# Value sums divided in the tail by spread inverse denominators, stacked rows sent one transfer at a time, and gate rows in three buffers

## The chip, the cores and the metric

The kernel runs on one core of a Trainium2 chip. The time is device time in microseconds (us), the median of several executions of the whole program. One execution is also recorded by the hardware profiler; it gives the rows quoted below. Engines are called by the profile's names: PE (matrix products; PEld is its weight load), DVE (vector), ACT (scalar), POOL (GpSimd), SP (the queue that issues nearly all DMAs here). A queue runs its instructions in order: an instruction that waits holds up all that stand behind it on the same queue.

## The reference, cut to what matters

```
g = sigmoid((x * gate_w).sum(-1, keepdims=True))           # x: 2048 x 512
qkv = x @ wqkv;  H = 32 heads, Dh = 16, window W = 256
scores = q k^T * Dh**-0.5, kept where 0 <= i - j < 256
o = softmax(scores) @ v                                      # per head
a = o.reshape(2048, 512) @ wo
b = (silu(x @ w_gate) * (x @ w_up)) @ w_down                 # F = 1792
return g * a + (1 - g) * b
```

A softmax is a sum of exponentials times values, divided by the sum of the exponentials. The kernel obtains both sums from the same matrix product: every head's values carry one more column of ones, so that of the 32 rows of a head in the result 16 are value sums and row 16 (`DH`) is the denominator.

## The kernel before

All products are made from pairs of fp32r halves (a high part and a remainder, `split`, three matmuls for one). 2048 tokens are 16 blocks of 128 (`NB`) or 4 chunks of 512 (`NCH`); the 32 heads are 8 groups of 4 (`G`); the 1792 hidden columns are 14 tiles (`NF`) with a gate and an up half each, 28 units.

1. Prologue (to about 127 us): x and the weights are loaded and split, V is made and stored to DRAM (`vd`), and Q and K are made for all groups by a product scheme with fewer multiplications. Each Q/K piece goes to a DRAM buffer (`xd`).

2. Lead-in, 64 ticks (about 127 to 188 us). A tick is one pass of the emitting loop: three steps of the FFN stream (`stream`, `unit`, `lanes`, matmuls at L483, copies of finished sums to SBUF tiles `ev` at L510 on ACT, stores to DRAM `raws` at L511 on SP) and, from tick 10 on, pieces of `stage1` of group 0 (row maxima of the scores, L539 on PE, L541 on DVE). Beside it the rows of Q and K are brought back from `xd` into tiles of stacked operands by `stack`: 12 DMAs of 128 KB for each half of a group, issued on SP at L320 and L322. The ring of `ev` tiles has `EV` = 5 buffers (`kept`).

3. Main part, 8 groups of 64 ticks (about 188 to 660 us). In group g each tick holds a quarter of `stage1` of group g + 1, a quarter of `stage2` of group g (scores again, L578, exponentials on ACT, L580, masks on POOL, L582 and L585) and 9/4 FFN steps on average. Every 16 ticks `av` makes the value sums of one chunk (L602), and `evacuate` moves them: PSUM tile `second` by ACT to `ob` (L615), PSUM tile `first` by DVE to `oe` (L616), their sum by POOL into `ob` (L619). `ob` has one buffer. `finish` divides, one chunk later, beside the evacuation of the next chunk: ahead of it DVE transposes 32 x 32 blocks of `ob` (L626), inverts the denominators (L629) and multiplies (L630), and two ticks behind it DVE transposes back into `oe` (L633) and POOL stores `oe` to DRAM `od` (L634). So the next copy into `ob` (L615 on ACT) waits for L626 on DVE. FFN steps around `av` are (2, 1, none, 2) at the four ticks and 4 right after `av`.

4. In the last group there is no `stage1`. In its place 8 of the 14 down weights are loaded into slots that have become free (`wd_early`, through `kept()` tiles, split by DVE 4 ticks later), three hidden tiles are begun (`tile_load`, `tile_early`, L694 on ACT), and the gates are made: `gate_block` loads 128 rows of x into the tile `xn` (L667, 256 KB) and 3 ticks later multiplies them with `gw` and sums on DVE (L668), 16 times. `xn` has one buffer, and the loads begin 5 ticks ahead of the last group.

5. Tail (about 660 us to the end). `step` multiplies the 14 hidden tiles of each chunk with the down weights, 12 matmuls of 128 x 512 a step (L79 to L81). For each step SP loads 512 KB of `raws` (`got`, L830), ACT and DVE make the hidden tile (L835, L836) and split it (L67, L70). During the first chunk the other six down weights and the four parts of `wo` are loaded through `raw2` (3 buffers) and split. `load_oc` brings back the attention output from `od` (L795); `attn_split` and `attn_out` project it, chunk 0 during chunk 1 and each later chunk at its own end. SP and DVE run ahead of PE by at most the buffers of `got` (4) and `hp` (3).

The order on every queue is the order of emission; `at(k, f)` and `later(n, f)` put work at a tick.

## Time and profile before

| | us |
|---|---|
| median of 3 runs | 868.2 (866.72 to 868.23) |
| the profiled execution, its own time | 870.03 |
| its span, first to last instruction | 868.0 |
| PE / DVE / ACT / POOL busy in the span | 834.5 / 579.1 / 465.5 / 376.0 |
| mean granted clock of PE | 0.986 |

A view by stretches gives, for a stretch of the span, the busy time of each engine with the number of its instructions, then the granted PE clock (1.00 is full), the mean share of the DMA engines and the rate. A timeline row is: start, duration, engine, line, operation, out<-in, count, and in brackets how long the engine had been idle before it and what ended the wait. A row of waits is: who waited <- for what: us in total, times, longest. A row of a group is: line, engine, operation, tiles, shapes, count | busy us in total, mean ns of one | idle time before. A row of the chain of waits has only start, duration, and what.

### The profile page before, as it was taken

To read this page: it belongs to the slowest core of one execution; us is meant where nothing else is said; L and a number is where in the kernel's file an instruction comes from. 1 tells how busy PE (TensorE), PEld (TensorE's weight loads), DVE (VectorE), ACT (ScalarE), POOL (GpSimd) and SP (SyncE) were. 2 spreads that over 40 slices of the span, in tenths; PEclk is the share of its full clock that TensorE was granted. 3 is DMA by queue.
4 is the path that set the end of the run, shared out by engine and by line. 5 is a ranking of instruction groups with operands and counts; after the bars stand their busy time and mean duration, and the time that the engine had idled before them with its cause. 6 is when DMAs were issued, how large, how long until landed. Compare 5 with 4: busy or idle time off the path is not lost.

```text
span 868.0 us, 20987 instructions
## 1 busy us (share of the span) xinstructions
PE 834.5 (96%) x7897; PEld 687.4 (79%) x7897; DVE 579.1 (67%) x1504; ACT 465.5 (54%) x947; POOL 376.0 (43%) x667
## 2 busy tenths in 40 slices
PE   9999999699999999999999999997878899999998
PEld 7888887598787788878887878785757688888886
DVE  5665524477888888888888888883665855254543
ACT  7455541136666676666675766664545453334341
POOL 5124465025656575565665655654643121102010
PEclk9999999899999999999999999999888999999999
DMA  8346678642544456345543554345556886375561
GB/s 297 128 169 235 249 259 279 203 136 84 175 149 160 134 167 201 109 158 177 171 156 118 187 177 135 130 129 178 167 176 222 291 269 206 100 242 169 179 185 48
DMA packets 78820, 154.20 MB, mean 178 GB/s; under 512 B 12352, under 2 KB 16832, under 8 KB 78720
## 3 DMA queue, kind: packets, MB, share of 16 engines
q1 hardware_dynamic: 74752, 138.97, 49.6%
q0 software_dynamic: 3968, 13.90, 4.3%
q8 instruction: 62, 1.02, 0.6%
q14 instruction: 38, 0.31, 0.1%
HBM read 88.34 MB, written 64.49 MB: 176 GB/s over the span
## 4 chain that ended last, share of the span: by engine, by line
PE 80%; DMA 5%; DVE 5%; POOL 3%; SPq 2%; issue 2%; ACT 1%; DVEq 0%; POOLq 0%; ACTq 0%
PE pb L483 15%; PE pa L483 15%; PE ps L602 8%; PE ps L539 6%; PE ps L81 5%; PE ps L79 5%; PE ps L80 5%; PE ps L578 4%; DMA xn<-xn 3%; PE ps L368 3%; PE ps L208 3%; PE pa L368 2%; PE pb L368 2%; PE pb L79 2%; PE pb L80 2%
## 5 line engine op out<-in xcount | busy, mean ns | idle before, releaser
L541 DVE CUSTOM_DVE_ANT_0 ps<-ps,mask 128x384 f32<-128x384 f32 (+2 forms) x512 | 269.8, 545 | 73.4 <-PE ps L539 28.9
L580 ACT ACTIVATE pt<-ps 128x384 f32<-128x384 f32 (+2 forms) x512 | 234.4, 478 | 99.9 <-PE ps L578 55.1
L578 PE MATMUL ps<-q,k 64*128 64x384 f32 (+2 forms) x512 | 166.7, 346 | 13.9 <-ACT pt L580 13.7
L539 PE MATMUL ps<-k,q 63*128 63x384 f32 (+2 forms) x512 | 163.1, 336 | 2.9 <-DVE mx L541 0.6
L582 POOL TENSOR_SCALAR_AFFINE_SELECT pt<-pt 128x256 f32<-128x256 f32 x256 | 106.9, 417 | 118.6 <-ACT pt L580 116.2
L539 PEld LDWEIGHTS ps<-k,q 63*128 63x128 f32 x512 | 92.4, 184 | 31.7 <-DVE mx L541 22.8
L578 PEld LDWEIGHTS ps<-q,k 64*128 64x128 f32 x512 | 94.2, 186 | 25.8 <-ACT pt L580 19.9
L483 PE MATMUL pb<-xhi,wh 64*128 64x512 f32 x432 | 106.8, 409 | 5.3 <-ACT ev L510 5.3
L483 PE MATMUL pa<-xhi,wh 64*128 64x512 f32 x432 | 104.8, 407 | 1.6 <-ACT ev L510 1.6
L483 PE MATMUL pb<-xlo,wh 64*128 64x512 f32 x432 | 105.2, 400 | 0.0
L483 PE MATMUL pb<-xhi,wl 64*128 64x512 f32 x432 | 103.8, 397 | 0.0
L483 PE MATMUL pa<-xlo,wh 64*128 64x512 f32 x432 | 102.6, 398 | 0.0
L483 PE MATMUL pa<-xhi,wl 64*128 64x512 f32 x432 | 100.7, 395 | 0.0
L585 POOL TENSOR_SCALAR_AFFINE_SELECT pt<-pt 128x256 f32<-128x256 f32 x224 | 96.0, 429 | 0.0
L836 DVE TENSOR_TENSOR sg<-got,sg 128x512 f32<-128x512 f32 x53 | 47.6, 898 | 70.4 <-ACT sg L835 57.7
L602 PE MATMUL ps<-pt,vg 64*32 64x320 f32 (+4 forms) x2816 | 77.7, 350 | 0.0
L602 PEld LDWEIGHTS ps<-pt,vg 64*32 64x32 f32 x2816 | 50.8, 106 | 28.4 <-issue 10.4
L619 POOL TENSOR_TENSOR ob<-oe,ob 128x512 f32<-128x512 f32 x32 | 41.8, 1306 | 71.1 <-DVE oe L616 56.1
L541 DVE DVE_READ_ACCUMULATOR2_ANT mx<- 128x1 f32 x512 | 72.2, 141 | 0.0
L483 PEld LDWEIGHTS pb<-xhi,wh 64*128 64x128 f32 x432 | 56.6, 188 | 11.6 <-ACT ev L510 6.2
L483 PEld LDWEIGHTS pa<-xhi,wh 64*128 64x128 f32 x432 | 54.3, 189 | 7.3 <-issue 3.0
L483 PEld LDWEIGHTS pb<-xhi,wl 64*128 64x128 f32 x432 | 57.5, 188 | 3.1
(230 smaller groups left out, 1683.9 us busy)
## 6 DMA issues: line engine op xcount, KB each, us to landing
raws<-ev SPq DMA_DIRECT2D x112, 256.0 KB
got<-raws SPq DMA_DIRECT2D x106, 256.0 KB
q<-xd SPq DMA_DIRECT2D x96, 128.0 KB
k<-xd SPq DMA_DIRECT2D x96, 128.0 KB
xd<-cx SPq DMA_DIRECT2D x16, 512.0 KB
xd<-cy SPq DMA_DIRECT2D x16, 512.0 KB
od<-oe POOLq DMA_DIRECT2D x32, 256.0 KB, 3.1
raw<-wgu SPq DMA_DIRECT2D x28, 256.0 KB
```

The costliest lines, as they stand in the source:

```text
L79: nc.tensor.matmul(ps, lh, rh, start=start and i == 0, stop=False, skip_group_check=skip)
L80: nc.tensor.matmul(ps, lh, rl, start=False, stop=False, skip_group_check=skip)
L368: nc.tensor.matmul(ps, l[:, w], r[:, k], start=n in (1, 2, 5) and k == m == 0, stop=k == 1 and m == 2, skip_group_check=True)
L483: mm = nc.tensor.matmul(ps[me], w[r], x[r], start=not second and i == 0, stop=bool(second) and i == n - 1)
L539: nc.tensor.matmul(ps[:, :n], QT[g % 2][pr][r, q0:q0 + P], KT[g % 2][pr][r, k0:k0 + n], start=True, stop=True)
L541: mx = nc.vector.tensor_tensor_reduce(out=ps[:, :n], in0=ps[:, :n], in1=mask[:, 3 * P - n:], scale=1.0, scalar=NEG, op0=ALU.add, op1=ALU.m ...
L578: nc.tensor.matmul(ps[:, :n], KT[g % 2][pr][r, k0:k0 + P], QT[g % 2][pr][r, k0:k0 + n], start=True, stop=True)
L580: BEHIND.append(nc.scalar.activation(pt[:, j, :n], ps[:, :n], AF.Exp, scale=SCALE))
L582: nc.gpsimd.affine_select(out=pt[:, :, :P], in_=pt[:, :, :P], pattern=[[0, 2], [1, P]], compare_op=ALU.is_ge, fill=0.0, base=0, channel_mu ...
L585: nc.gpsimd.affine_select(out=pt[:, :, 2 * P:], in_=pt[:, :, 2 * P:], pattern=[[0, 2], [-1, P]], compare_op=ALU.is_ge, fill=0.0, base=-1, ...
L602: nc.tensor.matmul(AV[g, c][h][32 * j:32 * j + 32, q0 - c * CH:q1 - c * CH], VG[4 * g + kb // 4][o, kb % 4, 17 * j:17 * j + 32], PT[g, kb, ...
L836: nc.vector.tensor_tensor(out=sg, in0=gu[1], in1=sg, op=ALU.mult)
```

## The change

- `finish` is gone. `evacuate` adds the two parts into `oe`, and POOL stores the undivided sums with their denominators to `od` at once.
- In the tail the denominators of a chunk (32 heads x 512) are loaded as a 128 x 128 tile (`load_den`, 64 KB), inverted by DVE (`put_den`), stored to DRAM (`rd`, 64 KB), and loaded back with each row repeated for the 16 rows of its head (`load_rd`, four DMAs of 256 KB a chunk, into the tiles of x that are no longer used). `attn_split` multiplies on DVE before it splits. `load_den` and `put_den` stand at steps 4 to 8 of the first chunk, `load_rd` beside each `load_oc`.
- `stack` yields after each DMA, and `spread` issues one DMA every tick or every second tick.
- `EV` is 7 in place of 5.
- The gates' rows go into three quarters of the slot `k01`, which is free in the last group; the loads begin one tick into that group, one every 3 ticks, and the products come 6 ticks after their load. Down weights 6 and 7, which had that slot, are loaded at ticks 54 and 58 of the group.
- The FFN steps around `av` are (2, 1, 2, 2) and 2 right after it.

```diff
@@ -26,7 +26,7 @@
 NSLOT = 4
 NEG = -1.0e30
 SCALE = DH ** -0.5
-EV = 5
+EV = 7
 SYNC = mybir.DependencyInfo(mybir.DependencyClass.Sync, mybir.DependencyReason.DATA)
 
 
@@ -47,6 +47,7 @@
     vd = dram.tile([G, P, NB, VW], F32, name="vd")
     od = dram.tile([G, P, S], F32, name="od")
     raws = dram.tile([NF, 2, NCH, P, CH], F32, name="raws")
+    rd = dram.tile([NCH, H, CH], F32, name="rd")
     xd = [[dram.tile([2, P, 2 * CH], F32, name=f"xd{g}{hf}") for hf in range(2)] for g in range(G)]
 
     gate = const.tile([P, NB], F32, name="gate")
@@ -318,8 +319,10 @@
             q, k = (halves_of(t[g % 2][pr])[hf] for t in (QT, KT))
             for b, w in enumerate((0, 1, 0)):
                 nc.sync.dma_start(q[b::4].bitcast(F32), xd[g][hf][w, 32 * pr:32 * pr + 32])
+                yield
             for b, w in enumerate((0, 0, 1)):
                 nc.sync.dma_start(k[b::4].bitcast(F32), xd[g][hf][w, 64 + 32 * pr:96 + 32 * pr])
+                yield
 
     SOON, AT_PRODUCT = {}, [0]
 
@@ -424,9 +427,9 @@
                     if i == j:
                         constant_rows(0, 0, (name,), nc.gpsimd)
                 if i == 7:
-                    stack(0, 0, (0,))
+                    run(stack(0, 0, (0,)))
                 if i == 11:
-                    stack(0, 0, (1,))
+                    run(stack(0, 0, (1,)))
                 if i == 10:
                     prepare()
             step_end()
@@ -458,6 +461,9 @@
 
         def at(k, *fs):
             AT.setdefault(k, []).extend(fs)
+
+        def spread(k, n, gen):
+            at(k, lambda: None if next(gen, run) is run else spread(k + n, n, gen))
 
         def tick_end():
             for f in AT.pop(NOW[0], ()):
@@ -604,35 +610,16 @@
                                          PT[g, kb, j // 2][o, j % 2, q0 - kb * P:q1 - kb * P],
                                          start=n == 0, stop=n == len(orders[0]) - 1, skip_group_check=True)
 
-        AB = {}
-
         def evacuate(g, c):
 
             first, second = AV[g, c]
             lo = 0 if c else 64
             e = osb.tile([P, CH], F32, name="oe", bufs=2)
-            b = osb.tile([P, CH], F32, name="ob")
-            nc.scalar.copy(b[:, lo:], second[:, lo:])
+            o = osb.tile([P, CH], F32, name="ob")
+            nc.scalar.copy(o[:, lo:], second[:, lo:])
             nc.vector.tensor_copy(e, first)
-            if lo:
-                nc.gpsimd.memset(b[:, :lo], 0.0)
-            nc.gpsimd.tensor_tensor(out=b, in0=e, in1=b, op=ALU.add)
-            AB[g, c] = e, b
-
-        def finish(g, c):
-
-            e, b = AB.pop((g, c))
-            ot = osb.tile([P, CH], F32, name="ot")
-            nc.vector.transpose(ot, b)
-            v = ot.rearrange("p (s e) -> p s e", e=32)
-            rc = osb.tile([P, CH // 32], F32, name="rc")
-            nc.vector.reciprocal(rc, v[:, :, DH])
-            nc.vector.tensor_tensor(out=v[:, :, :DH], in0=v[:, :, :DH],
-                                    in1=rc[:, :, None].to_broadcast([P, CH // 32, DH]), op=ALU.mult)
-            yield
-            nc.vector.transpose(e, ot)
+            nc.gpsimd.tensor_tensor(out=e[:, lo:], in0=e[:, lo:], in1=o[:, lo:], op=ALU.add)
             nc.gpsimd.dma_start(od[g, :, c * CH:(c + 1) * CH], e)
-            yield
 
 
 
@@ -647,11 +634,14 @@
             run(steps, 3)
             if n == 1:
                 constant_rows(1, 0, ("q00", "k00", "q01", "k01"), nc.gpsimd)
-                stack(0, 1)
+                spread(n - TICKS + 1, 1, stack(0, 1))
             if n in (8, 10, 12, 14):
                 hf, pr = divmod(n // 2 - 4, 2)
                 constant_rows(hf, 1, (f"q1{pr}", f"k1{pr}"), nc.gpsimd)
-                stack(1, hf, (pr,))
+            if n == 15:
+                spread(n - TICKS + 1, 2, stack(1, 0))
+            if n == 40:
+                spread(n - TICKS + 1, 2, stack(1, 1))
             if n == 40:
                 put_max(0, 0)
             if n >= 48 and n % 4 == 0:
@@ -660,12 +650,16 @@
         run(first)
         put_max(0, 1)
 
-        gwb = osb.tile([P, D], F32, name="gwb")
+        GT = []
+
+        def gate_place():
+            GT.extend(h for piece in halves_of(slot("k01", F32)) for h in halves_of(piece))
+            nc.sync.dma_start(GT[0], gw[None, :].to_broadcast([P, D]))
 
         def gate_block(b):
-            t = osb.tile([P, D], F32, name="xn")
+            gwb, t = GT[0], GT[1 + b % 3]
             nc.sync.dma_start(t, xn[b * P:(b + 1) * P])
-            later(3, lambda: nc.vector.scalar_tensor_tensor(t, t, 1.0, gwb, op0=ALU.mult, op1=ALU.mult,
+            later(6, lambda: nc.vector.scalar_tensor_tensor(t, t, 1.0, gwb, op0=ALU.mult, op1=ALU.mult,
                                                             accum_out=gate[:, b:b + 1]))
 
         def gate_end():
@@ -714,23 +708,23 @@
 
         at(4 * g7, put_pieces)
         for m in range(8):
-            wd_early(4 * (g7 + 1 + m + m // 4 * 1) + 2, m, m)
+            wd_early(4 * (g7 + 1 + m + m // 6 * 6) + 2, m, m)
         for n in range(2):
             at(4 * (g7 + 9) + 3 + 2 * n, lambda n=n: tile_load(n, RAW_AT[n]))
         early = tile_early(0)
         for n in range(6):
             at(4 * (g7 + 10) + 3 + 3 * n, lambda: run(early, 1))
         at(4 * (g7 + NB - 2) + 3, lambda: tile_load(2, RAW_AT[0]))
-        at(4 * g7 - 6, lambda: nc.sync.dma_start(gwb, gw[None, :].to_broadcast([P, D])))
+        at(4 * g7, gate_place)
         for b in range(NB):
-            at(4 * g7 - 5 + 4 * b - b // 4, lambda b=b: gate_block(b))
+            at(4 * g7 + 1 + 3 * b, lambda b=b: gate_block(b))
+        at(4 * (g7 + 13) + 1, lambda: pieces.__setitem__(slice(6, 8), halves_of(slot("k01"))))
         at(4 * (g7 + NB - 1), gate_end)
 
         for g in range(G - 2):
-            at(4 * (16 * g + 9) + 3, lambda g=g: stack(g + 2, 0))
-            at(4 * (16 * g + 17) + 1, lambda g=g: stack(g + 2, 1))
-
-        FIN = iter(())
+            spread(4 * (16 * g + 9) + 3, 1, stack(g + 2, 0))
+            spread(4 * (16 * g + 17) + 1, 1, stack(g + 2, 1))
+
         for t in range(G * NB + 1):
             g, i = divmod(t, NB)
             d, part = divmod(t, NSLOT)
@@ -746,20 +740,15 @@
                     run(s2, 2)
                 if t == G * NB and hd == 0:
                     tile_silu(1)
-                n = (2, 1, 4, 2)[hd] if values else (k + 1) * 9 // 4 - k * 9 // 4
-                if t < G * NB and not (values and hd == 2):
+                n = (2, 1, 2, 2)[hd] if values else (k + 1) * 9 // 4 - k * 9 // 4
+                if t < G * NB:
                     run(steps, n)
                 tick_end()
                 if hd == 1 and values:
                     av(*divmod(d - 1, NCH))
-                    run(FIN, 1)
                     evacuate(*divmod(d - 1, NCH))
                     if t < G * NB:
-                        run(steps, 4)
-                if hd == 3 and part == 0:
-                    run(FIN)
-                    if t:
-                        FIN = finish(*divmod(d - 1, NCH))
+                        run(steps, 2)
             if i in (7, 15) and g + 1 < G:
                 put_max(g + 1, i // 8)
             if t >= 10 and t % 4 == 2 and t + 6 < G * NB:
@@ -768,7 +757,6 @@
             for f in AT[k]:
                 f()
         tile_silu(2)
-        run(FIN)
 
     with ExitStack() as B:
         hp = B.enter_context(tc.tile_pool(name="hp", bufs=3, side="right"))
@@ -794,9 +782,26 @@
             heads = od[2 * k:2 * k + 2].rearrange("g (j e) s -> (g j) e s", e=32)
             nc.sync.dma_start(OC[c][:, k], heads[:, :DH, c * CH:(c + 1) * CH])
 
+        DEN = wop.tile([P, NCH, P], F32, name="den")
+        shares = od.rearrange("g (j e) s -> (g j) e s", e=32)[:, DH]
+
+        def load_den(c):
+            nc.sync.dma_start(DEN[:, c], shares[:, c * CH:(c + 1) * CH].rearrange("h (q i) -> h q i", q=4))
+
+        def put_den(c):
+            nc.vector.reciprocal(DEN[:, c], DEN[:, c])
+            nc.sync.dma_start(rd[c].rearrange("h (q i) -> (h q) i", q=4), DEN[:, c])
+
+        RD = [t.bitcast(F32) for c in range(2, 4) for t in (xhi[c], xlo[c])]
+
+        def load_rd(c, k):
+            nc.sync.dma_start(RD[c][:, k], rd[c, 8 * k:8 * k + 8][:, None].to_broadcast([8, DH, CH]))
+
         def attn_split(c, b):
             oh, ol = (by_k(bp.tile([P, D], F32R, name=w)) for w in ("oh", "ol"))
-            split(oh, ol, OC[c][:, :, b * P:(b + 1) * P], *act)
+            o, cols = by_k(raw2()), slice(b * P, (b + 1) * P)
+            nc.vector.tensor_tensor(out=o, in0=OC[c][:, :, cols], in1=RD[c][:, :, cols], op=ALU.mult)
+            split(oh, ol, o, *act)
             return oh, ol
 
         def attn_out(c, b, ohl):
@@ -898,10 +903,16 @@
                 waiting.append(halved(*fresh.pop(0)))
             for f in todo:
                 f()
+            if c == 0 and 4 <= n < 8:
+                load_den(n - 4)
+            if c == 0 and 5 <= n < 9:
+                put_den(n - 5)
             if c == 0 and n >= NF - 4:
                 load_oc(0, n - NF + 4)
+                load_rd(0, n - NF + 4)
             if c and 1 <= n < 5:
                 load_oc(c, n - 1)
+                load_rd(c, n - 1)
             if c == 1 and 2 <= n < 8:
                 attn_step(0, n - 2)
             if c and n >= 8:
```

## The prediction

> **What bounds the kernel now.** I read the page's slices first, then the time by stretches, then PE's timeline for its idle gaps, and last the waits of whoever ended each gap. The slices are fortieths of the span, 21.7 us each:
>
> ```profile
> PE   9999999699999999999999999997878899999998
> PEclk9999999899999999999999999999888999999999
> ```
>
> PE is busy nearly everywhere except in slice 8 and in slices 29 to 33, and its clock drops in the same places. By stretches (PE, PEld, DVE, ACT, POOL busy, then granted clock, DMA share, GB/s):
>
> ```profile
> 138.50:168.00 29.50, 22.33 (x170) 18.23 (x172) 16.24 (x65) 5.52 (x10) 5.85 (x6) 0.88 0.73 231
> 200.00:587.60 387.60, 385.34 (x5279) 315.13 (x5275) 318.89 (x1028) 255.95 (x565) 232.14 (x488) 1.00 0.48 152
> 587.60:601.10 13.50, 13.38 (x159) 10.58 (x154) 4.67 (x10) 8.95 (x20) 10.11 (x19) 1.00 0.54 162
> 587.60:660.30 72.70, 58.84 (x701) 47.45 (x696) 38.76 (x72) 36.71 (x84) 37.81 (x69) 0.91 0.54 169
> 660.30:662.54 2.24, 0.00 (x1) 0.01 (x1) 1.98 (x5) 1.78 (x5) 0.00 (x0) 1.00 0.34 134
> 662.54:692.50 29.96, 27.69 (x111) 21.82 (x112) 22.37 (x37) 12.37 (x22) 4.91 (x5) 0.94 0.88 295
> 692.50:712.00 19.50, 19.49 (x86) 15.78 (x86) 11.91 (x15) 12.50 (x22) 5.72 (x4) 1.00 0.93 278
> 712.00:868.00 156.00, 152.13 (x673) 125.53 (x671) 70.45 (x94) 57.18 (x101) 18.72 (x14) 1.00 0.51 163
> 810.95:812.25 1.30, 1.30 (x8) 1.07 (x7) 0.00 (x0) 0.35 (x1) 0.00 (x0) 1.00 0.44 159
> ```
>
> From 200 to 587.6 PE idles 2.3 us in 387.6: PE is the bound there, and freeing another engine can win at most those 2.3 us. The removable time lies in two places: 7.2 us idle in 138.5:168 and 13.9 us in the last group (587.6:660.3), each with a lowered clock on top.
>
> The first place, SP's queue, PE's three gaps, and ACT's wait:
>
> ```profile
> 149.57 1.81 SPq L322 DMA_DIRECT2D k<-xd  x3
> 151.50 0.52 SPq L511 DMA_DIRECT2D raws<-ev  x1
> 155.86 0.53 SPq L511 DMA_DIRECT2D raws<-ev  x1
> 161.14 0.60 SPq L511 DMA_DIRECT2D raws<-ev  x1
> 155.03 0.49 PE L483 MATMUL pa<-xhi,wh 64*128 64x512 f32 x1 [1.56 <-ACT ev L510]
> 160.74 0.70 PE L483 MATMUL pb<-xhi,wh 64*128 64x512 f32 x1 [2.16 <-ACT ev L510]
> 164.62 0.79 PE L483 MATMUL pb<-xhi,wh 64*128 64x512 f32 x1 [3.18 <-ACT ev L510]
> ACT ev L510 <- DMA raws<-ev: 12.2, 3, 5.1
> ```
>
> A stacked-row DMA costs SP 0.6 us of issue. They stand in packs ahead of the stores that free the five `ev` tiles; the copies wait for a tile, and PE for the copies.
>
> The second place, PE's four gaps and ACT's waits, then DVE's:
>
> ```profile
> 608.75 1.06 PE L578 MATMUL ps<-q,k 64*128 64x384 f32 x2 [5.83 <-ACT pt L580]
> 626.57 0.82 PE L578 MATMUL ps<-q,k 64*128 64x384 f32 x2 [1.92 <-ACT pt L580]
> 636.98 0.82 PE L578 MATMUL ps<-q,k 64*128 64x384 f32 x2 [3.16 <-ACT pt L580]
> 648.45 0.97 PE L578 MATMUL ps<-q,k 64*128 64x384 f32 x2 [2.81 <-ACT pt L580]
> 607.77 0.53 ACT L615 COPY ob<-ps 128x448 f32<-128x448 f32 x1 [7.38 <-DVE ot L626]
> 625.54 0.59 ACT L615 COPY ob<-ps 128x512 f32<-128x512 f32 x1 [5.00 <-DVE ot L626]
> 635.43 0.63 ACT L694 ACTIVATE ev<-k 128x512 f32<-128x512 f32 x1 [3.34 <-DMA k<-raws]
> 647.42 0.58 ACT L615 COPY ob<-ps 128x512 f32<-128x512 f32 x1 [7.45 <-DVE ot L626]
> DVE xn L668 <- DMA xn<-xn: 21.5, 10, 3.0
> ```
>
> Three of the four gaps are one chain: with a single `xn`, load and product alternate, so DVE waits 21.5 us for rows; the transpose that frees `ob` stands behind these waits; ACT's copy waits for the transpose, the exponentials behind the copy wait too, and PE runs out of PSUM. The gap at 636.98 is another: ACT waits for the load of a hidden tile.
>
> **The change part by part.**
>
> *Stacked rows one at a time, EV 7: -8.* In the lead-in the stores no longer stand behind 24 DMAs x 0.6 us = 14 us of issue but behind one or two (1.2 us), and two more tiles are free. The bound of the gain is the 7.2 us idle plus PE's half-speed work after the last gap: clock 0.88 over 29.5 us is 3.5 us, of which about 1.5 us lie on work. Together 8.7; at worst one gap stays: -5. I take -8, near the upper end, because every gap has the same cause. The DMAs needed soonest, the second half of group 0, still go out first; SP is not full when spread (36 x 0.6 = 22 us in 60). In the main part the packs cover nothing that PE waits for: 0.
>
> *Division out of the main part: 0.* Removed are the first three of these rows (the other two are for the tail):
>
> ```profile
> L626 DVE STREAM_TRANSPOSE ot<-ob 128x512 f32<-128x512 f32 x32 | 22.5, 703 | 0.0
> L630 DVE TENSOR_TENSOR ot<-ot,rc 128x256 f32<-128x256 f32 x32 | 13.7, 427 | 1.1
> L629 DVE RECIPROCAL rc<-ot 128x16 f32<-128x16 f32 x32 | 8.1, 254 | 1.1
> L696 DVE RECIPROCAL ev<-ev 128x512 f32<-128x512 f32 x1 | 3.3, 3348 | 0.0
> L836 DVE TENSOR_TENSOR sg<-got,sg 128x512 f32<-128x512 f32 x53 | 47.6, 898 | 70.4 <-ACT sg L835 57.7
> ```
>
> With the second transpose that is about 2.1 us x 32 = 67 us off DVE, beside PE in 28 of the 32. Between 0 and -2.3. POOL's sum and store stay, the store now right behind the sum. The steps moved from behind `av` put the same four steps between `av` and the second pair of scores that follows it, so the two PSUM copies keep their 1.1 us of cover; without it a chunk would lose up to one such copy, 0.59 us by L615 above. I take 0.
>
> *Gates in three buffers, no transpose, in the last group: -15.* The first chunk of that group ran nearly without a gap at clock 1.00 in 13.5 us, and its value sums are the short ones:
>
> ```profile
> 599.21 1.95 PE L602 MATMUL ps<-pt,vg 64*32 64x320 f32 x64
> 620.34 2.55 PE L602 MATMUL ps<-pt,vg 64*32 64x320 f32 x96
> ```
>
> Four such chunks, the later three with 0.6 us more, are 55.8 against 72.7: -17. Idle (13.9) plus the clock's loss (0.09 x 72.7 = 6.5, partly idle too) would allow -20. What is late next is the tile load at 636.98, whose emission is not moved: I leave 2 of its 3.2 us. Then -15. The products run 6 ticks (about 5 us) after their load, with three loads in flight. A transfer that is late now delays DVE but no longer holds `ob`, which POOL frees. At the other end, if waits for down-weight or row loads take DVE's place again, half remains: -8.
>
> *Change to the tail: -1.5.* DVE no longer does 2 x 2.1 us of division around 661 to 669, ahead of the work that opens the tail.
>
> ```profile
> 661.90 0.58 ACT L615 COPY ob<-ps 128x512 f32<-128x512 f32 x1 [0.46 <-DVE ot L626]
> ```
>
> The 2.24 us gap at 660.3 shrinks by this 0.46 at most; the 1.51 us gap at 674.59 below should go. Two weights loaded late take back a part. Between -3 and +1.
>
> *Division in the tail: +4.* Three prices. (a) DVE: 4 inversions of 128 x 128. From 254 ns for 16 columns and 3348 for 512, a straight line gives 0.95 us each, 3.8 together, in steps 5 to 8, while DVE is 75% busy and PE already waits for it now and then; 16 products of 128 x 512 (0.9 us each, as L836) fall where DVE is under half busy: 0. (b) SP: four stores wait for DVE, with the loads of later steps behind them; these have about three steps' lead. (c) Transfers: 16 x 256 KB + 8 x 64 KB = 4.5 MB. Of these 2.5 MB fall in 662 to 712, where the DMA share is already 0.88 and 0.93; at 295 GB/s they need 8.5 us, and about 5 of the 49.5 us are free: 3.5 over. After 712 the share is 0.51: free. What stands against full cover in that stretch:
>
> ```profile
> 674.59 0.50 PE L81 MATMUL ps<-q,hl 128*128 128x512 f32 x1 [1.51 <-DVE hl L70]
> 685.93 0.50 PE L81 MATMUL ps<-k,hl 128*128 128x512 f32 x1 [0.15 <-DVE hl L70]
> 692.26 0.50 PE L81 MATMUL ps<-q,hl 128*128 128x512 f32 x1 [0.60 <-DVE hl L70]
> 700.24 0.62 ACT L67 CAST woh<-raw 128x512 fp32r<-128x512 f32 x1 [4.41 <-DMA raw<-wo]
> ```
>
> The hidden tiles reach PE just in time or late, and ACT waits 4.41 us for a transfer. Lower end 0 (`got` has four buffers), upper end 12. I take +4, the 3.5 of transfers and a little for the inversions.
>
> The repeated rows have an outermost dimension of 8, like the loads from `od`. In 810.95:812.25, where only such a load moves, the DMA share is 0.44 at 159 GB/s: half the engines. The Trainium skill, page "DMA: Bandwidth & Descriptors", section "Rules for kernel authors", says why: an outermost dimension below 16 confines a DMA to at most that many engines. The row agrees; it makes the second rival below.
>
> **Sum.** -8 + 0 - 15 - 1.5 + 4 = -20.5 on an execution of 870.0, so 849.5. The median of the runs, 868.2, is 0.2% below that execution; from it, 847.7. I predict 848.
>
> **Rivals.** *Everything covered:* the tail costs nothing and the last group reaches -18: 868.2 - 8 - 18 - 2.5 = about 840. For it: SP and DVE may run three steps ahead. Against it: the zero slack at 685 to 701.
>
> *Half the engines:* 2 MB of repeated rows in the crowded stretch on half the engines at 159 GB/s need 12.6 us instead of the 6.8 at 295, six more: 854. For it the 0.44 share; against it, other loads can fill the other half.
>
> *The wait moves:* the last group's waits pass to the loads of down weights and tiles, -8 in place of -15: 855. For it: 4 MB of gate rows are now packed into fewer microseconds and the gap at 636.98 has this form; against it the share of 0.54.
>
> *Slower:* the 4.5 MB of the tail are not hidden at all. At 159 GB/s that is 28 us, with the inversions 32, against 24.5 gained: 875. It decides as soon as over three quarters of the added transfers delay PE. Against it the share of 0.51 after 712.
>
> *No effect:* the gaps are closed and reopened elsewhere in equal measure, 868.
>
> **How the numbers follow.** Forecast (843 to 852) 0.53, covered 0.15, half engines 0.17, wait moves 0.08, slower 0.05, no effect 0.02. The range 837 to 857 leaves out the slower and unchanged cases and the far parts of the first two rivals. Faster, by over 0.2% (1.7 us, about what can be told from no change): 0.93; same 0.02; slower 0.05.
>
> **What would show it.** PE gaps between 153 and 165 gone, clock 1.00 there. In the last group no copy from PSUM on ACT that waits for DVE, under 4 us idle on PE, and the stretch near 57 us. From 200 us to that group the same 387 us. In the tail's first 50 us new waits on DVE or ACT for the denominators, repeated rows, `wo` or `got`, worth about 4 us on PE. I am wrong if the tail's idle time passes 10 us, or if the last group keeps 65 us.

## The result, and the profile after

The changed kernel takes 841.4 us (median of 4 runs, 838.62 to 841.71) against 868.1 us (4 runs, 866.72 to 868.23): a ratio of 0.969, with a 95% interval of 0.967 to 0.971. Its profiled execution took 841.71 us with a span of 840.0. The forecast was 848, with a range of 837 to 857.

The slices of the page of the changed kernel (fortieths, now 21 us each):

```profile
PE   9999999999999999999999999999979799999988
PEclk9999999999999999999999999999999899999999
```

The low clock around 160 us and the shallow slices of the last group are gone. New are two shallow slices, 30 (609 to 630 us) and 32 (651 to 672 us); the tail begins in the first of them. The stretches (PE, PEld, DVE, ACT, POOL busy, then clock, DMA share, GB/s), first the lead-in's old place of trouble, then the main part, the last group, and the tail in three pieces:

```profile
138.50:168.00 29.50, 29.50 (x263) 26.57 (x263) 24.14 (x90) 6.76 (x13) 7.11 (x7) 1.00 0.69 224
189.40:558.70 369.30, 369.30 (x5177) 320.43 (x5175) 277.80 (x916) 256.98 (x561) 227.03 (x479) 1.00 0.48 158
558.70:612.40 53.70, 52.39 (x698) 42.05 (x695) 33.16 (x58) 35.29 (x83) 38.88 (x70) 1.00 0.69 235
612.40:618.00 5.60, 3.95 (x110) 2.76 (x107) 4.40 (x10) 4.81 (x10) 0.78 (x2) 1.00 0.28 106
618.00:666.90 48.90, 38.75 (x156) 29.98 (x156) 26.35 (x40) 16.77 (x30) 6.73 (x6) 0.94 0.81 257
666.90:840.00 173.10, 164.87 (x711) 133.71 (x711) 86.23 (x118) 65.77 (x115) 20.98 (x17) 0.98 0.58 184
```

To set the kernels side by side, each span is cut where PE's queue of weight loads reaches the line of `av`, with its wait for a semaphore: at group 0, chunk 0; at group 6, chunk 3; and at group 7, chunk 3. The four pieces are called lead-in (with all that stands ahead of it), main part, last group and tail. These cuts lie 1 to 1.5 us ahead of the first weight loads and matrix products of `av`; the expectations quoted below count from the products, so that the tail is 226.2 us in them where the table has 227.6.

| us | lead-in ends | main part | last group | tail | span |
|---|---|---|---|---|---|
| before | 199.9 | 384.1 | 72.3 | 211.7 | 868.0 |
| after | 189.4 | 369.3 | 53.7 | 227.6 | 840.0 |
| difference | -10.5 | -14.8 | -18.6 | +15.9 | -28.0 |
| predicted | -8 | 0 | -15 | +2.5 | -20.5 |

Two places came out near the forecast. Two did not: the main part gave 14.8 us where 0 stood, and the tail took 15.9 where 2.5 stood (+4 and -1.5).

Each piece is read from one profiled execution, and it scatters. Among the kernels below that leave a piece as it is in the changed kernel, the lead-in ends at 189.4 to 190.9, the main part takes 369.1 to 369.9, the last group 52.3 to 55.4, and the tail 225.5 to 227.6. A difference within these ranges says nothing.

### The profile page after: what moved, and what is told of

The parts are those of the page before. It is cut to its first block, busy times and chain, and to the rows that moved or that the text cites. A ratio compares the mean times of both kernels' runs of the same rounds, so it can differ in the third digit from the quotient of the medians.

```text
span 840.0 us, 20730 instructions
## 1 busy us (share of the span) xinstructions
PE 816.7 (97%) x7897; PEld 687.6 (82%) x7897; DVE 542.8 (65%) x1396; ACT 468.3 (56%) x947; POOL 370.9 (44%) x659
## 5 line engine op out<-in xcount | busy, mean ns | idle before, releaser
L545 PE MATMUL ps<-k,q 63*128 63x384 f32 (+2 forms) x512 | 157.4, 327 | 0.0
L489 PE MATMUL pb<-xhi,wh 64*128 64x512 f32 x432 | 99.3, 402 | 0.0
L489 PE MATMUL pb<-xlo,wh 64*128 64x512 f32 x432 | 98.1, 394 | 0.0
L489 PE MATMUL pa<-xhi,wh 64*128 64x512 f32 x432 | 98.0, 400 | 0.0
L489 PE MATMUL pb<-xhi,wl 64*128 64x512 f32 x432 | 97.4, 392 | 0.0
L489 PE MATMUL pa<-xlo,wh 64*128 64x512 f32 x432 | 96.3, 394 | 0.0
L489 PE MATMUL pa<-xhi,wl 64*128 64x512 f32 x432 | 95.6, 392 | 0.0
L71 POOL TENSOR_TENSOR ol<-raw,oh 128x512 fp32r<-128x512 f32 x16 | 20.7, 1295 | 132.5 <-ACT oh L68 132.5
L547 DVE DVE_READ_ACCUMULATOR2_ANT mx<- 128x1 f32 x512 | 72.3, 141 | 0.0
L621 POOL TENSOR_TENSOR oe<-oe,ob 128x512 f32<-128x512 f32 (+1 forms) x32 | 41.0, 1281 | 65.3 <-ACT ob L619 57.6
L620 DVE COPY oe<-ps 128x512 f32<-128x512 f32 x32 | 22.1, 691 | 61.7 <-issue 44.1
```

The source lines that it names most:

```text
L489: mm = nc.tensor.matmul(ps[me], w[r], x[r], start=not second and i == 0, stop=bool(second) and i == n - 1)
L545: nc.tensor.matmul(ps[:, :n], QT[g % 2][pr][r, q0:q0 + P], KT[g % 2][pr][r, k0:k0 + n], start=True, stop=True)
L547: mx = nc.vector.tensor_tensor_reduce(out=ps[:, :n], in0=ps[:, :n], in1=mask[:, 3 * P - n:], scale=1.0, scalar=NEG, op0=ALU.add, op1=ALU.m ...
```

## The experiments

**Where the main part's 14.8 us come from.** The first pair of runs puts the FFN steps around the value sums back into the changed kernel, and puts the new placement alone into the kernel before. The diff is that of the first; the second is its reverse.

```diff
-                n = (2, 1, 2, 2)[hd] if values else (k + 1) * 9 // 4 - k * 9 // 4
-                if t < G * NB:
+                n = (2, 1, 4, 2)[hd] if values else (k + 1) * 9 // 4 - k * 9 // 4
+                if t < G * NB and not (values and hd == 2):
...
-                        run(steps, 2)
+                        run(steps, 4)
```

> The changed kernel with the FFN steps around the value sums as before: (2, 1, none, 2) and 4 right behind. It asks where the 14.9 us between the first value sums of group 0 and those of group 6, chunk 3 went (384.3 us before, 369.4 after; I had put this part at 0). Theory placement (two steps between the value sums and the second pair of scores hide a wait inside the busy rows of PE): the stretch returns to about 384 and the time to about 856. Theory division (DVE and the hold on ob were in PE's way, about 0.5 us a chunk): the stretch stays at 369 to 371 and the time within 2 us of 841.4. Theory spread stacks: likewise no change here.

> The kernel before with only the new placement of FFN steps: (2, 1, 2, 2) and 2 right behind the value sums. Theory placement: the stretch from the first value sums of group 0 to those of group 6, chunk 3 falls from 384.3 to about 370 and the time from 868.1 to about 853 to 855. Theory division, or spread stacks: the stretch stays near 384, the time near 868.

Measured: steps as before 850.4 us (ratio to before 0.977, 0.974 to 0.981), main part 378.2; new placement alone 860.1 us (0.989, 0.986 to 0.992), main part 376.0. Both say that the placement is worth 8 to 9 us and is not all. For the rest, two runs: the changed kernel with the division put back (`finish`, `FIN` and the use of `ob` as before, nothing of `den` and `rd`), and the changed kernel with the packs of stacked rows.

```diff
-            o, cols = by_k(raw2()), slice(b * P, (b + 1) * P)
-            nc.vector.tensor_tensor(out=o, in0=OC[c][:, :, cols], in1=RD[c][:, :, cols], op=ALU.mult)
-            split(oh, ol, o, *act)
+            split(oh, ol, OC[c][:, :, b * P:(b + 1) * P], *act)
```

```diff
-                spread(n - TICKS + 1, 1, stack(0, 1))
+                run(stack(0, 1))
...
-            spread(4 * (16 * g + 9) + 3, 1, stack(g + 2, 0))
+            at(4 * (16 * g + 9) + 3, lambda g=g: run(stack(g + 2, 0)))
```

> The changed kernel with the division put back where it was (in the main part on DVE, no work in the tail): spread stacks, EV 7, gates in three buffers and the new placement of FFN steps stay. The two placements already run put 8 to 9 of the 14.9 us of the main part down to the steps; 6 to 7 are open. Theory division (DVE's 2.1 us a chunk, or its hold on ob, cost PE 0.2 us a chunk): the stretch from the first value sums to those of group 6, chunk 3 is 376, the last group about 55, the tail about 210, the time about 831 to 834. Theory stacks or ev tiles: the stretch is 369 to 370 and the time about 826. By the prediction's terms (tail +4, main part 0) the time would be about 837 to 839.

> The changed kernel with the stacked rows sent in packs again, in the lead-in and in the main part; EV stays 7. Theory packs (SP's 0.6 us a transfer ahead of the stores causes the lead-in's gaps): the first value sums come at 196 to 201 in place of 190.4. Theory ev tiles (two more buffers cover the packs): within 1.5 us of 190.4. For the main part: if the packs cost PE the 6 to 7 us that the steps do not explain, the stretch returns from 369.4 to about 376; if the division does, it stays at 369 to 370.

Measured: division put back 835.1 us (0.961, 0.958 to 0.963), main part 375.7, tail 211.9; packs put back 842.9 us (0.970, 0.967 to 0.973), main part 369.7, lead-in's end at 192.4. So the division off DVE is worth 6.4 us in the main part, and the packs nothing there.

The row that tells why is in the waits of the weight loads, in the main part of each kernel. (Who waited <- for what: us in total, times, longest; PEld is PE's weight load.) Before, then the new placement alone, then the steps put back, then the division put back:

```profile
PEld ps L539 <- DVE mx L541: 21.2, 47, 0.5
```
```profile
PEld ps L539 <- DVE mx L541: 9.4, 20, 0.5
```
```profile
PEld ps L545 <- DVE mx L547: 11.8, 27, 0.5
```
```profile
PEld ps L544 <- DVE mx L546: 9.4, 20, 0.5
```

In the changed kernel no such row is left. The scores of `stage1` wait for a PSUM tile that DVE frees when it has taken the row maxima. Against the changed kernel's main part of 369.3, the four are 14.8, 6.7, 8.9 and 6.4 us longer: 0.68 to 0.75 us for each us of this wait. One chunk of the kernel before shows two such waits (first PE and PEld, then DVE with PEld):

```profile
317.72 0.39 PE L483 MATMUL pb<-xlo,wh 64*128 64x512 f32 x2
317.95 0.40 PE L483 MATMUL pb<-xhi,wl 64*128 64x512 f32 x2
318.42 0.18 PEld L539 LDWEIGHTS ps<-k,q 63*128 63x128 f32 x1 [0.51 <-DVE mx L541]
...
318.74 0.70 DVE L633 STREAM_TRANSPOSE oe<-ot 128x512 f32<-128x512 f32 x1
319.37 0.53 DVE L541 CUSTOM_DVE_ANT_0 ps<-ps,mask 128x384 f32<-128x384 f32 x1
320.01 0.18 PEld L539 LDWEIGHTS ps<-k,q 63*128 63x128 f32 x1 [0.47 <-DVE mx L541]
```

In the second, the division's last transpose stands ahead of the row maxima on DVE; in the first, none does. Of the 47 waits before, 20 (9.4 us) end 1.27 us behind the start of such a transpose, and 27 (11.8 us) have none just ahead of them. Putting the steps back leaves the 27 without a transpose and none of the others; with the new placement and the division, in either of the two kernels, the 20 behind a transpose are left. So each half of the change removes its own set. The hold on `ob` plays no part: in this stretch of the kernel before no wait of ACT for DVE's transpose is listed.

The first wait also shows why PE looked busy. A pair of products of the FFN starts 0.23 us behind the one before it and has rows of 0.39 to 0.40 us. Here the next product starts 0.47 us after the last, and the last one's row covers all but 0.07 of that.

The page had the wait as one row before and has nearly all of it gone after:

```profile
L539 PEld LDWEIGHTS ps<-k,q 63*128 63x128 f32 x512 | 92.4, 184 | 31.7 <-DVE mx L541 22.8
```
```profile
L545 PEld LDWEIGHTS ps<-k,q 63*128 63x128 f32 x512 | 89.0, 184 | 11.7 <-DVE mx L547 0.9
```

**The lead-in.** Both parts of the change were predicted as one, and the runs show that either does it. With neither (the new placement alone) the lead-in ends at 201.4; with EV 7 and packs at 192.4; with spread rows and EV 5 (the single-buffer run, below) at 190.2; with both at 189.4 to 190.9 in the kernels that have them.

**The last group.** Three buffers, or the freed `ob`? The run goes back to one buffer and the old places, without the old hold; for room the `ev` tiles are five again:

```diff
-EV = 7
+EV = 5
...
-            gwb, t = GT[0], GT[1 + b % 3]
+            t = osb.tile([P, D], F32, name="xn")
...
-            at(4 * g7 + 1 + 3 * b, lambda b=b: gate_block(b))
+            at(4 * g7 - 5 + 4 * b - b // 4, lambda b=b: gate_block(b))
```

> The changed kernel with the gates' rows in a single buffer, at the places before (products 3 ticks behind a load), down weights as before, EV 5 for room; there is no transpose that holds ob. It asks what closed the last group's gaps: the three buffers, or that POOL, not DVE, frees ob. Theory buffers (DVE's waits for rows reach PE by themselves, through the hidden tiles and the weights that DVE splits): the last group stays at 62 to 72 us (72.6 before, 54.0 after). Theory hold (only through ob did DVE's waits reach PE): the last group is 54 to 57 us although DVE waits 15 to 20 us for rows.

Measured: 852.1 us (0.981, 0.978 to 0.984), last group 65.1. DVE's wait for rows is that of before (21.5), and PE has two large gaps:

```profile
DVE xn L658 <- DMA xn<-xn: 21.3, 11, 3.3
```
```profile
587.33 1.07 PE L584 MATMUL ps<-q,k 64*128 64x384 f32 x2 [5.20 <-ACT pt L586]
610.51 1.06 PE L584 MATMUL ps<-q,k 64*128 64x384 f32 x2 [4.17 <-ACT pt L586]
```

Ahead of these gaps ACT had waited for transfers, and not for DVE:

```profile
586.30 0.58 ACT L516 COPY ev<-pb 128x512 f32<-128x512 f32 x1 [5.16 <-DMA raws<-ev]
608.96 0.63 ACT L684 ACTIVATE ev<-k 128x512 f32<-128x512 f32 x1 [4.33 <-DMA k<-raws]
```

Both transfers are issued by SP, and with a single buffer SP cannot issue the next load of rows until DVE is done with the last. SP's waits for that, in the last group of this run, of the kernel before, and of the changed kernel (where the buffer is called `k`):

```profile
SPq L657 <- DVE xn L658: 35.1, 13, 4.0
```
```profile
SPq L667 <- DVE xn L668: 38.8, 12, 5.4
```
```profile
SPq L661 <- DVE k L662: 10.2, 7, 3.3
```

So the single buffer reached PE in two ways: through DVE's hold on `ob`, as predicted, and through SP's queue, where stores that free `ev` tiles and loads of hidden tiles stand behind the rows. The gap at 636.98 in the kernel before, which the prediction had set apart, is of the second kind. The load that ACT waited for there was issued right behind a load of rows that SP had held up:

```profile
625.24 0.42 SPq L276 DMA_DIRECT2D ev<-wd  x1
630.07 0.33 SPq L667 DMA_DIRECT2D xn<-xn  x1
630.45 0.43 SPq L276 DMA_DIRECT2D ev<-wd  x1
630.97 0.99 SPq L689 DMA_DIRECT2D k<-raws  x2
```

With the hold kept and three buffers (the run with the division put back) the group takes 55.5. So, beside the rest of the change, three buffers alone give 55.5, the freed `ob` alone 65.1, both 53.7, against 72.3 before. The buffers are worth most of it. The 1.8 us between 55.5 and 53.7 lie within the scatter, and how much of the 65.1 is owed to the five `ev` tiles was not tried. In the changed kernel PE has two gaps left in that group, and neither is at a tile load, for which 2 us had been left over in the forecast:

```profile
589.17 0.32 PE L608 MATMUL ps<-pt,vg 64*32 64x64 f32 x8 [0.39 <-POOL pt L588]
590.34 0.53 PE L608 MATMUL ps<-pt,vg 64*32 64x64 f32 x22 [0.85 <-POOL pt L588]
```

**What the tail pays for.** The larger of PE's gaps in the tail of the changed kernel, with what ACT and DVE waited for, and the pieces of the chain of waits there (start, duration, what):

```profile
618.03 0.50 PE L80 MATMUL ps<-q,k 128*128 128x512 f32 x1 [1.68 <-ACT ob L619]
630.07 0.60 PE L82 MATMUL ps<-q,hl 128*128 128x512 f32 x1 [3.14 <-DVE hl L71]
666.91 0.80 PE L80 MATMUL ps<-k,hh 128*128 128x512 f32 x1 [5.62 <-ACT hh L68]
...
751.99 0.50 PE L80 MATMUL ps<-k,hh 128*128 128x512 f32 x1 [0.81 <-ACT hh L68]
...
665.20 0.62 ACT L68 CAST woh<-raw 128x512 fp32r<-128x512 f32 x1 [8.86 <-DMA raw<-wo]
627.66 0.43 DVE L70 CAST q<-raw 128x512 fp32r<-128x512 f32 x1 [4.55 <-DMA raw<-wd]
```
```profile
621.30 6.14 DMA raw<-wd
656.86 10.17 DMA got<-raws
796.84 8.58 DMA got<-raws
```

At 666.91 ACT has stood 8.86 us at a `wo` part that came late, with the hidden tile that PE needs behind it on its queue. The `wo` part is not the only transfer that was late: the chain of waits goes by a load of `got` issued at 656.86, which took 10.17 us. First the two runs that tell the bytes from the engines that carry them: denominators twice in DRAM for loads on 16 engines, and no repeated rows (that kernel leaves the division out).

```diff
-    rd = dram.tile([NCH, H, CH], F32, name="rd")
+    rd = dram.tile([NCH, H, 2, CH], F32, name="rd")
...
-            nc.sync.dma_start(RD[c][:, k], rd[c, 8 * k:8 * k + 8][:, None].to_broadcast([8, DH, CH]))
+            nc.sync.dma_start(RD[c][:, k], rd[c, 8 * k:8 * k + 8].rearrange("h r s -> (h r) s")[:, None].to_broadcast([16, DH // 2, CH]))
```

```diff
-            nc.vector.tensor_tensor(out=o, in0=OC[c][:, :, cols], in1=RD[c][:, :, cols], op=ALU.mult)
+            nc.vector.tensor_tensor(out=o, in0=OC[c][:, :, cols], in1=OC[c][:, :, cols], op=ALU.mult)
...
-                load_rd(0, n - NF + 4)
...
-                load_rd(c, n - 1)
```

> The changed kernel with the inverse denominators stored twice in DRAM (8 more stores of 64 KB in all: two for each chunk in place of one), so that each repeated-row load has an outermost dimension of 16 and not of 8; the bytes loaded are the same. It asks why the tail grew by 15.9 us from the last value sums to the end (210.3 before, 226.2 after), where I had put 2.5. Theory half the engines (a load with 8 outermost rows uses 8 of the 16 DMA engines): the tail falls by 4 to 8 us to 218 to 222, the time to 833 to 837. Theory bytes (4.5 MB more in a crowded stretch, whichever engines carry them): within 2 us of 841.4. Theory order (what delays PE is where the loads stand on SP's queue, ahead of the wo loads): also within 2 us.

> The changed kernel without the 16 loads of repeated rows (4 MB); the product on DVE stays but multiplies the value sums with themselves, so the division by the denominators is left out of the result. Denominators are still loaded, inverted and stored. Theory transfers (the repeated rows delay the loads of got and wo): the tail falls from 226.2 to about 213 to 216, the time to 828 to 831. Theory DVE (the inversions and products delay PE): the tail stays above 222, the time above 837. By the prediction's own terms the transfers were 3.5 of 4 us, so about 838.

Measured: 16 engines 840.2 us (0.965, 0.963 to 0.968; the interval overlaps that of the changed kernel), tail 226.3, down 1.3, which is within the scatter; no repeated rows 829.9 us (0.954, 0.952 to 0.956), tail 215.7, down 12.0. The crowded stretch in the changed kernel, with 16 engines, and with no repeated rows:

```profile
650.00:662.00 12.00, 11.02 (x46) 8.48 (x46) 4.32 (x6) 2.87 (x6) 1.30 (x1) 1.00 0.83 233
662.00:675.00 13.00, 7.86 (x25) 5.91 (x26) 4.43 (x6) 6.59 (x11) 1.27 (x1) 0.74 0.72 229
```
```profile
650.00:662.00 12.00, 11.07 (x46) 8.20 (x46) 6.32 (x8) 4.87 (x9) 2.52 (x2) 1.00 1.00 258
662.00:675.00 13.00, 8.39 (x29) 6.16 (x29) 3.86 (x6) 6.60 (x11) 1.27 (x1) 0.87 0.86 251
```
```profile
662.00:675.00 13.00, 12.27 (x53) 9.81 (x54) 7.83 (x11) 8.14 (x14) 2.77 (x3) 1.00 0.86 253
```

With the wider loads the share of the engines rises from 0.83 to 1.00. The Trainium skill, page "DMA: Bandwidth & Descriptors", section "Rules for kernel authors", says that an outermost dimension under 16 confines a DMA to at most that many engines; the trace agrees by this rise. But the rate rises only from 233 to 258 GB/s, and the gap behind is still 3.88 us where it was 5.62. The repeated rows as such account for 12.0 of the 15.9 us. What remains to ask is whether their bytes or their place cost it. Three runs change only places. First the loads spread over the steps (`PLAN` lists them, from step 9 on about one for each step, with s = 14 * c + n), and, in a run of its own, the down weights one step later:

```diff
-            if c == 0 and n >= NF - 4:
-                load_oc(0, n - NF + 4)
-                load_rd(0, n - NF + 4)
-            if c and 1 <= n < 5:
-                load_oc(c, n - 1)
-                load_rd(c, n - 1)
-            if c == 1 and 2 <= n < 8:
-                attn_step(0, n - 2)
+            for f, cc, k in PLAN.get(s, ()):
+                f(cc, k)
+            if c == 1 and 3 <= n < 9:
+                attn_step(0, n - 3)
```

```diff
-        ready = [load_wd(8, pieces[8], raw2())]
+        ready = []
...
-            if c == 0 and 2 <= n < NF - 6:
-                ready.append(load_wd(n + 6, pieces[n + 6], raw2()))
+            if c == 0 and n < NF - 5:
+                ready.append(load_wd(n + 5, pieces[n + 5], raw2()))
```

> The changed kernel with the 32 tail loads of value sums and repeated rows issued about one for each step from step 9 on, in place of two for each step in four packs, and the projection of chunk 0 one step later. Same bytes, same engines. Theory crowding (the loads of a pack delay got and wo for a few steps, and the clock drops behind the gap): the tail falls from 226 to 214 to 218 us and the time to 829 to 833. Theory bytes (the added 4.5 MB cost wherever they stand): within 3 us of 841. Without those loads at all the time was 829.9.

> The changed kernel with the tail's six loads of down weights begun one step later (weight 8 is no longer loaded and split ahead of the second hidden tile). It asks what the gap of 3.1 to 3.6 us some 12 us into the tail is, which stays when the repeated rows' loads are left out or spread. Theory order (DVE waits 4.6 us for a down weight that PE needs five steps later, with the first hidden tile's lower half behind it): the gap falls under 1 us, the half-speed stretch at 630 goes, the tail shrinks by 3 to 5 us, the time to 836 to 839. Theory crowding (everything that moves there is needed): the gap stays within 1 us, the time within 1.5 us of 841.4.

Measured: spread 836.5 us (0.962, 0.960 to 0.964), tail 223.3, that is 4.3 us less where 8 to 12 were expected; down weights later 839.8 us (0.967, 0.963 to 0.971; not to be told from the changed kernel), tail 226.2, where 3 to 5 us less were expected. Both moved gaps more than they closed them (start and duration of PE's next product, and in brackets the gap ahead of it). With the loads spread, chunk 0 is still crowded, and a gap of 1.97 us stands 9 us earlier; with the weights later the gap at 630 is gone, and the large one has stayed:

```profile
631.03 0.50 PE L82 MATMUL ps<-q,hl 128*128 128x512 f32 x1 [3.10 <-DVE hl L71]
...
658.03 0.50 PE L80 MATMUL ps<-q,hh 128*128 128x512 f32 x1 [1.97 <-ACT hh L68]
```
```profile
632.83 0.50 PE L82 MATMUL ps<-k,hl 128*128 128x512 f32 x1 [0.23 <-DVE hl L71]
...
667.50 0.80 PE L80 MATMUL ps<-k,hh 128*128 128x512 f32 x1 [5.63 <-ACT hh L68]
```

The next pair takes the crowd out of chunk 0 altogether, in the changed kernel and in the one with the division put back. Down weights come one step later, as above; denominators are loaded at steps 5, 8, 11 and 15 and inverted two steps behind; value sums and repeated rows come about one a step from step 13 on (in the second kernel, value sums alone, about one every two steps); `wo` comes later, and so do the projections of chunks 0 and 1:

```diff
-            if c == 0 and n >= 6 and n % 2 == 0:
-                ready.append(load_wo((n - 6) // 2))
+            if c == 0 and n >= NF - 5 and n < NF - 1:
+                ready.append(load_wo(n - NF + 5))
...
-            if c == 1 and 2 <= n < 8:
-                attn_step(0, n - 2)
-            if c and n >= 8:
-                attn_step(c, n - 8)
+            if c == 2 and 2 <= n < 8:
+                attn_step(1, n - 2)
+            if c and n >= 8:
+                attn_step((0, 0, 2, 3)[c], n - 8)
```

> The changed kernel with a tail spread for its transfers: down weights one step later, denominators at steps 5, 8, 11 and 15 and inverted two steps behind, the loads of wo at steps 9 to 12, the loads of value sums and repeated rows one for each step from step 13 on, the projection of chunk 0 in the second half of chunk 1's steps and that of chunk 1 in the first half of chunk 2's. Theory crowding and order (nothing of the tail's 15.9 us is owed to the bytes): the tail comes down from 226 to 212 to 215 us, the time to 826 to 829, better than with the division left where it was (835.1). Theory bytes: not below 835.

> The kernel that keeps the division in the main part and has everything else of the change (835.1), with the same spread of the tail as far as it applies: down weights one step later, wo at steps 9 to 12, the loads of value sums about one for every two steps, the projections moved likewise. Its tail of 211.9 us holds gaps of 2.7 and 1.9 us and one half-speed stretch of 3.4. Expected: 2 to 5 us less, 830 to 833. If the division's place is a net gain once the tail is spread, this one is slower than the spread version of the changed kernel by 3 to 6 us; if not, it is level or faster.

Measured: 827.1 us (0.952, 0.947 to 0.956) with a tail of 213.0 for the first, and 831.9 us (0.957, 0.953 to 0.960) with a tail of 207.4 for the second; the runs of the two don't overlap (825.02 to 828.67, 829.84 to 832.91). The first has one larger gap left beside that at the tail's opening, at 682, and DVE's first product there is late, behind the last repeated rows of chunk 0. Two rows of its timeline, of DVE and of SP's queue (the first names a load of `got`, but the semaphore that DVE's queue waited for until 680.75 is that of the load in the second row):

```profile
680.89 0.69 DVE L803 TENSOR_TENSOR raw<-xhi,xhi 128x512 f32<-128x512 f32 x1 [3.37 <-DMA got<-raws]
...
671.70 0.59 SPq L798 DMA_DIRECT2D xhi<-rd  x1
```

The last run moves these loads, and one pair of denominator steps, ahead:

```diff
-        for cc, places in enumerate(((13, 14, 15, 16, 17, 18, 19, 20), (21, 22, 23, 24, 25, 26, 27, 28),
+        for cc, places in enumerate(((11, 12, 13, 14, 15, 16, 17, 18), (20, 21, 22, 23, 24, 25, 26, 27),
...
-            if s in (5, 8, 11, 15):
+            if s in (5, 8, 11, 14):
```

> The changed kernel with the spread tail (827.1), its loads for chunk 0 two steps earlier (from step 11), those for chunk 1 one step earlier, and the last pair of denominator steps one step earlier. In the spread version one gap of 2.2 us is left at 682, with half speed behind it: DVE's first product comes at 680.9, after the last repeated rows of chunk 0, which were issued at 671.7. Theory lead (these rows came too late by 2 to 4 us and nothing else is short): the gap goes, the tail falls from 213.0 to 209 to 211 us, the time to 823 to 825.5. Theory crowding (two steps earlier they meet the loads of wo and got again): the gap only moves, the time stays at 826 to 830.

Measured: 823.2 us (5 runs, 822.01 to 826.84; ratio 0.948, 0.946 to 0.950), tail 210.7. The stretch that had run at clock 0.74 with PE 60% busy is now nearly full, at about the rate of transfers without the repeated rows (253):

```profile
662.00:675.00 13.00, 12.80 (x55) 9.95 (x54) 6.11 (x10) 4.97 (x10) 0.00 (x0) 1.00 0.88 258
```

The tail with the division is now 1.0 us shorter than the tail before without it (211.7), though all 4.5 MB are still moved. So most of the 15.9 us was owed to the places of the work and its order on the queues, for what was moved includes the loads of weights and the projections. That the bytes cost nothing is not shown: the tail that was spread likewise and has no division takes 207.4, or 3.3 us less. How much of these 3.3 is real stays open, since the profiled execution here was the slowest of its five, 3.6 us above their median, and that of the other kernel the fastest of its four, 2.1 below. This version is the fastest of all that were run.

## Why the prediction was right and wrong

*Lead-in, -8:* right in mechanism, and 2.5 us short; the clock in the stretch is 1.00 and the three gaps are gone. The bound of 8.7 was too low. Compared weight load by weight load of the FFN, the changed kernel was already 0.8 us ahead at 140 us, and won 9.6 us between 151 and 171 us, just where the gaps were: 7.2 us idle with the whole 3.5 of the clock's loss, of which the bound had taken 1.5, make 10.7. Spread rows and more tiles were counted as one; either does nearly all of it.

*Division out of the main part, 0, and steps moved, 0:* wrong. The step that failed is "From 200 to 587.6 PE idles 2.3 us in 387.6: PE is the bound there, and freeing another engine can win at most those 2.3 us". PE's busy time is the union of the products' rows, and these overlap: a row of 0.4 us covers most of a stop where a pair of products should have started every 0.23 us. The division cost 6.4 us and the placement of the steps 8 to 9, and both appear as waits of PEld for DVE's row maxima. I looked for what the steps cover in PSUM copies on ACT, and not for what DVE gets done while they run.

*Last group, -15:* right in direction and in the buffers as the cause, 3.6 us short. The 2 us left for the tile load were not needed: that load was late because SP stood at a load of rows ahead of it, so the three buffers moved it too. Of the two ways from the single buffer to PE the prediction had the one through `ob` and missed the one through SP's queue. The rival in which waits pass to down weights and tiles did not come.

*Change to the tail, -1.5:* the gap at its opening shrank from 2.24 to 1.68, by 0.56 where at most 0.46 was said. But the gap behind it grew from 1.51 to 3.14, which the same sentence had going away: DVE now waits 4.55 us for a down weight with the hidden tile behind it.

*Division in the tail, +4:* far too small; with the division put back the tail is 15.7 us shorter. The inversions took 0.94 to 0.95 us, as estimated. The term that failed is (c): 8.5 us of transfers, of which 5 free, at 295 GB/s. Of that stretch, 650 to 675 us moved only 229 to 233 GB/s, and a late `wo` part held the hidden tile on ACT, so that a lack of some us became a stop of 5.6 us, with a clock of 0.74 from 662 to 675. "After 712 the share is 0.51: free" failed too: the packs of chunks 2 and 3 met the loads of hidden tiles, for gaps of 0.81 us and more. The rival of half the engines named the right loads, and its price for this part, 10 us, is the nearest to the 15.7 measured; but its reason is not borne out, as 16 engines give no gain that can be told from scatter. The slower rival's 32 us, in which nothing is hidden, are twice too many.

*The total:* 841.4 lies within the range, and near the case "everything covered" (840), but by luck and not for its reasons. The tail was not covered; the main part's gain of 14.8 paid for the 13.4 us by which the tail exceeded its term. Of the two conditions named for being wrong one was met: PE's idle time in the tail is 20 us (227.6 less 207.6 busy), over the 10 allowed. The last group did not keep 65 us. The sign that the main part would keep its 387 us failed as well.

One reading of the slices was off by one place: the shallow ones before are 28 to 32, not 29 to 33. Nothing was worked out from it.

And moving the division was not a gain as it was made: without that part the kernel takes 835.1 us in place of 841.4. With the tail spread the sign turns: 827.1 against 831.9, since the main part's gain is kept and the tail costs less than it.

## What to carry to other kernels

Before an engine is called the bound, look at what its weight loads waited for, and not at its busy share alone. Work that is moved into a stretch with free transfer time on average must be given places there: count the transfers a step, and look at what stands behind each one's consumer on its own queue. When a buffer is single, ask which queue stands still until it is free, and what else that queue carries. When several changes come together, take each away once, since one may be a loss that the others cover.

## What the runs showed that I had not expected

PE's busy time was 381.84 us of 384.10 in the main part before, and 14.8 us of it could still be removed, at 0.7 us for each us that PEld waited for DVE. The Trainium skill says as much, page "Trainium Kernel Development and Optimization", section "Performance Expectations": the busy time of products is a bad measure of how close a kernel is to its limit, because they are pipelined, and the busy share of the weight loads is a good one. The trace agrees: PEld was busy for 312.80 of 384.10 us before (81%) and for 320.43 of 369.30 after (87%).

```profile
199.90:584.00 384.10, 381.84 (x5176) 312.80 (x5173) 316.43 (x1020) 254.11 (x561) 230.97 (x485) 1.00 0.48 152
```

The engines' share does not tell the rate. At the tail's opening, where hidden tiles and down weights are loaded, a share of 1.00 moves 351 GB/s (changed kernel); with repeated rows on 16 engines, among other loads, a share of 1.00 moves 258. Why was not tried.

```profile
618.00:630.00 12.00, 8.91 (x38) 7.06 (x38) 5.04 (x8) 4.08 (x7) 1.85 (x2) 1.00 1.00 351
```
